# Chunked attention and an MLP on one core: exp stationary in the V products, a ones column for the sums, x normalized by token and turned, and a new order of the first three blocks

## The chip, the cores and the metric

One core of one Trainium2 chip. The metric is the device time of one execution in microseconds (us), median of several runs. The kernel runs on one core only. A profile is one execution of its own; its span is 1.8 us (before) below the time measured for that same execution.

## The reference, cut to what matters

```python
def _attn_ref(q, k, v):                       # (8, 8, 576, 64): batch, heads, tokens, head dim
    # 9 chunks of 64 tokens; each chunk attends to itself only
    scores = scale * np.matmul(q_c, k_c.transpose(0, 1, 2, 4, 3))
    scores = scores - np.max(scores, axis=-1, keepdims=True)
    attn = np.exp(scores)
    attn = attn / (np.sum(attn, axis=-1, keepdims=True) + 1e-09)
    return np.matmul(attn, v_c)...

def _moe_ref(x, w_in, w_out, beta):           # x (4608, 512), w_in (512, 2048), w_out (2048, 512)
    h = x @ w_in
    g = h * (1.0 / (1.0 + np.exp(-beta * h)))
    return g @ w_out

# x is the attention's output, token by token: row = token, column = 64 * head + d
```

## The kernel before

4608 tokens are nine blocks of 512. Per block: q and k are loaded, cast to bf16 and turned so that the head dimension lies on the partitions (by TensorE for blocks 0 to 2, by DMA from block 3 on); 64 score matmuls (8 heads x 8 chunks, each 64x64) fill four banks of PSUM, the memory that takes matmul results; ScalarE takes exp; 64 V products follow; the result is normalized. Then come 64 "first products" (w_in stationary, x moving, 512 columns), tanh on ScalarE and a gate on VectorE, and 64 "second products" with w_out. Of a matmul's two operands the stationary one is loaded by an instruction of its own (PEld in the profiles); the other is called the moving one. The first and second products are called dense matmuls here; each has 512 columns.

In before the V products give x with the head dimension on the partitions, as the first products want it. The sums over keys then have to be spread over those partitions:

```python
def sums(blk, bank):                  # 16 matmuls with a selector of ones
    for b in range(4):
        for hp in range(4):
            ... matmul(A[32*hp:32*hp+32, bank, 0:128], onesel[:, b, :], E[:, hp, 128*b:128*b+128], ...)

def invert(blk, bank):                # three steps on VectorE; the last two go from SBUF to SBUF
    reciprocal(R[:, :], A[:, bank, 0:128])
    tensor_copy(Rhi[:, :], R[:, :])                       # float32 -> bf16
    scalar_tensor_tensor(Rs, Rhi, mask, R, mult, subtract)

def spread(blk, u, banks):            # 8 matmuls: 1/sum to every partition of its head
    ... matmul(A[:, banks[g], col:col+128], sel[:, u, ..., :], Rs[:, :])

def attend(blk, u, banks):            # 32 V products, v stationary, exp moving
    ... matmul(ps[64*hb:64*hb+64, banks[g], col:col+64], v_bf[r, sa, cc, head, :], E[r, 2*u+hb, col:col+64])

def normalize(blk, u, g, bank):       # o_sb is a copy that ScalarE makes first
    tensor_tensor(xT[...], o_sb[...], A[:, bank, :], mult)
```

The kernel's own small scheduler puts all operations into one order by a "time" in slots, and each engine executes its part in that order. From block 2 on, a slot is one group of 4 first products and one of 4 second products of the block before.

Order of the first blocks in before: all first products of block 0, all second products of block 0 (with block 1's attention between them), all first products of block 1 (with block 2's attention), then first products of block n and second products of block n-1 alternate.

The softmax here doesn't subtract the row's maximum and nothing guards it: scores larger than these inputs give would overflow.

## Time and profile before

| | before |
|---|---|
| measured | 343.31 us median of 3 (341.46 to 345.04) |
| span of the profile | 342.2 us |
| first dense matmul / first of block 1 / first of block 2 | 22.8 / 64.8 / 97.6 us |
| block 2's stage (its first product to that of block 3) | 37.5 us |
| later blocks, one stage each | 32.6 us (block 7's, with the last block's scores, 31.8) |
| block 8's first product to the end | 45.0 us |

The stages are read from the weight loads of the first products, 64 to a block, in order of time. Lines of the page of before: the busy share of the engines; the span in 40 slices (each digit tenths of busy time; PEclk is the granted clock of TensorE); and the shares of the chain that ended last (the work that the end of the run waited for, followed back from step to step).

```profile
span 342.2 us, 6329 instructions
PE 303.8 (89%) x2688; PEld 148.3 (43%) x2688; DVE 150.8 (44%) x236; ACT 165.1 (48%) x262; POOL 113.2 (33%) x126
...
PE   1669978977589879999999999999999999999996
...
PEclk9999989999789999999999999999999999999999
...
PE 74%; DVE 11%; ACT 8%; DMA 3%; issue 2%; SPq 1%; POOL 0%; ACTq 0%; DVEq 0%; POOLq 0%
```

TensorE (PE) is the bottleneck nearly throughout, but 303.8 us of busy time is not all needed: 1152 dense matmuls at the 0.216 us at which they issue are 248.8 us.

PE waits 10.0 us in all for the inverted sums (`Rs`). And the two small VectorE steps L417 and L419 have means, 467 and 449 ns, that are far above their usual duration, as the timeline of VectorE shows for block 4 and for block 3:

```profile
152.72 0.95 DVE L415 RECIPROCAL R<-A 128x128 f32<-128x128 f32 x1
153.71 0.23 DVE L417 CAST Rhi<-R 128x128 bf16<-128x128 f32 x1
153.97 0.35 DVE L419 SCALAR_TENSOR_TENSOR Rs<-Rhi,mask,R 128x128 bf16<-128x128 bf16 x1
```

```profile
122.79 0.95 DVE L415 RECIPROCAL R<-A 128x128 f32<-128x128 f32 x1
123.78 1.40 DVE L417 CAST Rhi<-R 128x128 bf16<-128x128 f32 x1
125.21 0.35 DVE L419 SCALAR_TENSOR_TENSOR Rs<-Rhi,mask,R 128x128 bf16<-128x128 bf16 x1
```

The timeline of PE in before, in columns start, duration, what (a count after x; in brackets the idle time before it): the three long waits in block 2's stage, the last of them in block 3's attention; then the score burst of a usual block, and that of the last block.

```profile
99.51 0.60 PE L465 MATMUL F<-xT,w_in_bf 128*128 128x512 bf16 x2 [1.14 <-DVE xT L454]
...
119.19 0.41 PE L408 MATMUL A<-E,onesel 128*32 128x128 bf16 x16 [1.26 <-ACT E L402]
...
125.62 0.62 PE L429 MATMUL A<-Rs,sel 128*128 128x128 bf16 x8 [2.47 <-DVE Rs L419]
```

```profile
170.53 1.51 PE L395 MATMUL A<-qkO 64*64 64x64 bf16 x64
```

### The profile page before, as it was taken

How to read it: one execution, taken by the hardware profiler on the slowest of the kernel's cores; microseconds unless marked ns; L12 is line 12 of the kernel's file. 1: busy time of each engine (PE TensorE's matmuls, PEld its weight loads, DVE VectorE, ACT ScalarE, POOL GpSimd, SP SyncE). 2: the span in 40 equal slices, each digit the busy share in tenths (PEclk: the TensorE clock that was granted, in tenths of full speed). 3: DMA queues.
4: the chain of work that ended last, by engine and by line, in shares of the span. 5: the costliest groups of instructions: out<-in, count | busy, mean ns of one | idle time of the engine just before them, and what ended most of it. 6: DMA issues, size and time to landing. Idle time of an engine off the chain costs nothing.

```text
span 342.2 us, 6329 instructions
## 1 busy us (share of the span) xinstructions
PE 303.8 (89%) x2688; PEld 148.3 (43%) x2688; DVE 150.8 (44%) x236; ACT 165.1 (48%) x262; POOL 113.2 (33%) x126
## 2 busy tenths in 40 slices
PE   1669978977589879999999999999999999999996
PEld 1434435443234434545454454445444444444442
DVE  5255733184553355344534543463356336443300
ACT  2436633476234525465455546554655565544421
POOL 0467357242620960780096019403800000000000
PEclk9999989999789999999999999999999999999999
DMA  8999999999918979919932991450000000110012
GB/s 214 280 389 345 220 310 290 277 270 217 240 27 176 303 107 255 256 48 235 292 87 56 225 283 54 93 94 33 31 33 31 33 33 31 47 48 31 31 65 90
DMA packets 93484, 52.85 MB, mean 154 GB/s; under 512 B 66320, under 2 KB 84752, under 8 KB 93456
## 3 DMA queue, kind: packets, MB, share of 16 engines
q1 hardware_dynamic: 86208, 43.00, 50.6%
q10 hardware_dynamic: 7248, 9.45, 8.0%
q8 instruction: 21, 0.34, 0.4%
q14 instruction: 7, 0.06, 0.1%
HBM read 36.71 MB, written 9.44 MB: 135 GB/s over the span
## 4 chain that ended last, share of the span: by engine, by line
PE 74%; DVE 11%; ACT 8%; DMA 3%; issue 2%; SPq 1%; POOL 0%; ACTq 0%; DVEq 0%; POOLq 0%
PE F L465 33%; PE F L481 31%; ACT tt L471 4%; PE A L395 4%; DVE g L474 3%; PE A L429 3%; DVE R L415 2%; ACT E L402 2%; PE A L442 2%; DVE xT L454 1%; DMA qkstage<-in_k_dram 1%; SPq L285 1%; DVE Rhi L417 1%; DMA out_dram<-ostage 1%; DVE Rs L419 1%
## 5 line engine op out<-in xcount | busy, mean ns | idle before, releaser
L474 DVE SCALAR_TENSOR_TENSOR g<-tt,F 128x512 bf16<-128x512 bf16 x144 | 98.5, 686 | 148.6 <-ACT tt L471 148.6
L471 ACT ACTIVATE tt<-F,beta_half 128x512 bf16<-128x512 f32 x144 | 98.5, 687 | 113.9 <-PE F L465 113.0
L465 PE MATMUL F<-xT,w_in_bf 128*128 128x512 bf16 x576 | 150.1, 390 | 2.7 <-DVE xT L454 1.9
L481 PE MATMUL F<-w_out_bf,g 128*128 128x512 bf16 x576 | 144.8, 381 | 0.0
L465 PEld LDWEIGHTS F<-xT,w_in_bf 128*128 128x128 bf16 x576 | 55.4, 100 | 69.8 <-issue 5.4
L481 PEld LDWEIGHTS F<-w_out_bf,g 128*128 128x128 bf16 x576 | 54.9, 98 | 63.1 <-issue 0.6
L342 POOL COPY qkO<-qkT 128x1024 bf16<-128x1024 bf16 x22 | 42.6, 1980 | 92.7 <-PE A L395 84.3
L342 POOL CAST qkcast<-qkstage 128x1024 bf16<-128x1024 f32 x30 | 30.5, 1048 | 25.5 <-DMA qkstage<-in_k_dram 11.2
L486 ACT ACTIVATE ostage<-F 128x512 f32<-128x512 f32 x36 | 21.5, 597 | 23.7 <-PE F L481 21.5
L454 DVE TENSOR_TENSOR xT<-o_sb,A 128x512 bf16<-128x512 f32 x36 | 24.1, 681 | 2.5 <-PE A L429 2.3
L429 PE MATMUL A<-Rs,sel 128*128 128x128 bf16 x144 | 12.9, 239 | 13.0 <-DVE Rs L419 10.0
L449 ACT ACTIVATE o_sb<-A 128x512 f32<-128x512 f32 x32 | 18.8, 592 | 11.1 <-ACT ostage L486 4.2
L402 ACT ACTIVATE E<-A 128x512 bf16<-128x512 f32 x36 | 20.8, 595 | 5.9 <-PE A L395 3.4
L342 POOL CAST v_bf<-vstage 128x512 bf16<-128x512 f32 x36 | 21.3, 625 | 4.6 <-DMA vstage<-in_v_dram 4.5
L429 PEld LDWEIGHTS A<-Rs,sel 128*128 128x128 bf16 x144 | 9.8, 107 | 19.7 <-DVE Rs L419 14.0
L395 PE MATMUL A<-qkO 64*64 64x64 bf16 x576 | 12.9, 196 | 3.4 <-DVE qkO L342 2.2
L395 PEld LDWEIGHTS A<-qkO 64*64 64x64 bf16 x576 | 11.9, 110 | 7.1 <-issue 4.0
L415 DVE RECIPROCAL R<-A 128x128 f32<-128x128 f32 x9 | 8.6, 951 | 11.5 <-PE F L442 6.3
L369 PE MATMUL F<-identity,qkcast 128*128 128x128 bf16 x32 | 4.1, 311 | 8.7 <-DVE qkcast L342 6.9
L334 POOL CAST w_out_bf<-wstage 128x512 bf16<-128x512 f32 x16 | 9.7, 647 | 5.2 <-DMA wstage<-in_moe_w_out_dram 5.2
L322 POOL CAST w_in_bf<-wstage 128x512 bf16<-128x512 f32 x16 | 9.2, 617 | 4.6 <-DMA wstage<-in_moe_w_in_dram 4.6
L442 PEld LDWEIGHTS A<-E,v_bf 64*64 64x64 bf16 x512 | 5.9, 111 | 7.9 <-issue 3.8
(33 smaller groups left out, 66.4 us busy)
## 6 DMA issues: line engine op xcount, KB each, us to landing
out_dram<-ostage ACTq DMA_DIRECT2D x36, 256.0 KB, 2.3
qkstage<-in_q_dram SPq DMA_DIRECT2D x32, 256.0 KB, 4.2
qkstage<-in_k_dram SPq DMA_DIRECT2D x32, 256.0 KB, 5.7
vstage<-in_v_dram SPq DMA_DIRECT2D x32, 256.0 KB, 6.3
wstage<-in_moe_w_in_dram SPq DMA_DIRECT2D x4, 1024.0 KB, 10.2
wstage<-in_moe_w_out_dram SPq DMA_DIRECT2D x4, 1024.0 KB, 9.0
qkstage<-in_q_dram SPq DMA_DIRECT2D x8, 128.0 KB, 4.8
qkstage<-in_k_dram SPq DMA_DIRECT2D x8, 128.0 KB, 5.6
```

What stands on the lines that cost most here:

```text
L342: P.op(eng, lambda e: e.tensor_copy(dst, src), reads, writes)
L395: return e.matmul(A[64 * g:64 * g + 64, 2 * u + hb, col:col + 64], kT[r, 2 * cc + g, :], qT[r, 2 * cc + g, :])
L402: P.op("act", lambda e: e.activation(E[:, bank, :], A[:, bank, :], AF.Exp, scale=0.125), reads=[K("A", bank, v=("s", blk))], writes=[K("E" ...
L415: P.op("dve", lambda e: e.reciprocal(R[:, :], A[:, bank, 0:128]), reads=[K("A", bank, v=("l", blk))], writes=[K("R", v=blk)])
L429: return e.matmul(A[:, banks[g], col:col + 128], sel[:, u, 2 * (2 * w + ch) + g, :], Rs[:, :])
L449: P.op("act", lambda e: e.activation(o_sb[:, g, :], ps[:, bank, :], AF.Copy), reads=[K(psname, bank, v=("o", blk, u))], writes=[K("o_sb", ...
L454: P.op("dve", lambda e: e.tensor_tensor(xT[:, sx, 2 * u:2 * u + 2, :].rearrange("p w (c g i) -> p w c g i", c=4, g=2)[:, :, :, g, :], o_sb ...
L465: P.op("pe", lambda e, c=c: e.matmul(F[:, bank, :], w_in_bf[:, c, 128 * t:128 * t + 128], xT[:, sx, c, :], start=(c == 0), stop=(c == NC - ...
L471: P.op("act", lambda e: e.activation(tt[:, T % 3, :], F[:, bank, :], AF.Tanh, scale=beta_half[:, t:t + 1]), reads=[K("F", bank, v=("h", T) ...
L474: P.op("dve", lambda e: e.scalar_tensor_tensor(g2[:, sg, t, :], tt[:, T % 3, :], 1.0, F[:, bank, :], ALU.add, ALU.mult), reads=[K("F", ban ...
L481: P.op("pe", lambda e, t=t: e.matmul(F[:, bank, :], g2[:, sg, t, 128 * s:128 * s + 128], w_out_bf[:, t, :], start=(t == 0), stop=(t == NT ...
L486: P.op("act", lambda e: e.activation(ostage[:, N % NOS, :], F[:, bank, :], AF.Copy, scale=0.5), reads=[K("F", bank, v=("o", N))], writes=[ ...
```

## The change

Its intent: make exp the stationary operand, so that each V product gives tokens on the partitions; give v a 65th column of ones, so that the same product gives the sum too; then normalizing is one reciprocal of 16 columns and one multiply per half block, with no sums, no spreading and no copy. The price: x now has tokens on the partitions and must be turned, by TensorE in blocks 0 to 2 and by DMA from block 3 on. Besides, scores are issued as two bursts of 32, and the first three blocks come in a new order: block 1's q, k, v are loaded ahead of w_out, its attention goes under and after block 0's first products, and block 1's first products already alternate with block 0's second products.

```diff
-        v_bf = sb("v_bf", [128, NVA, 4, H, 64], BF16)
+        v_bf = sb("v_bf", [128, NVA, 4, H, 66], BF16)      # columns 64, 65 set to 1.0
-        def sums ... invert ... spread ... copy_o            (cut)
+        def attend(blk, u, ps=A, psname="A"):
+            ...   matmul(ps[64*half:64*half+64, bank, col:col+65],
+                         E[r, 2*u+hb, 256*w+64*cc:256*w+64*cc+64],
+                         v_bf[r, sa, cc, 4*u+2*w+hb, 0:65])
+        def normalize(blk, u, ps=A, psname="A"):
+            reciprocal(rec[:, u, :], o[:, :, :, 64])
+            tensor_tensor(x_sb[:, u, ...], o[:, :, :, 0:64], rec... broadcast over 64, mult)
+        def turn_dma(blk, u):  dma_start_transpose(xT[:, blk % NXT, u, ...], x_sb[:, u, ...])   # SP queue
+        def turn_pe(blk, u, ...):  8 transposes with the identity, then a copy by ACT or DVE
         def mm1(blk, t, bank):
-                    F[:, bank, :], w_in_bf[...], xT[:, sx, c, :],
+                    F[:, bank, :], w_in_bf[...], x_of(sx, c),       # runs of 64 columns
         (order)
-            return (0, 32)[blk] if blk < 2 else 16 * (blk + 1)
+            return 0 if blk == 0 else 16 * blk + 8
+        at(-43.5, load_qk, 1, 0) ... load_v, 1                       # ahead of w_out
-                at(t0, scores, blk, hp)
+                at(t0 + (hp // 2) * u, scores, blk, hp)
+                if blk > 2:  turn_dma   else:  turn_pe
         (other slots of the schedule cut)
```

## The prediction

> **What bounds it now.** TensorE. The chain of waits gives PE 74% of the 342.2 us span, DVE 11%, ACT 8%. In the timeline the 1152 dense matmuls issue every 0.216 us: 248.8 us, which the change does not touch. They run from 22.8 us to 339.0 us, so 67 us of that stretch is something else, in two parts.
>
> *Steady stage.* Scores of consecutive blocks start at 170.60, 203.19 and 235.78 us in the chain: 32.6 us a block, of which 128 dense matmuls are 27.6. Attention takes 4.95 us: scores about 1.55, two V products 0.5 each, sums 0.45, two spreads 0.55 each, and about 1.2 us in which PE waits (sums for exp 0.4-0.5, spread for the DVE inversion of 0.95+0.23+0.35 us). The score matmuls start four per 33 ns for the first 32 of 64, then one per 34 ns. The 32 of a V product all go at the fast rate. The Trainium skill (TensorE: Matmul & The Clock Gate, opening table) gives TensorE a queue of 64 instructions; 32 loads and 32 matmuls are just that. The trace agrees.
>
> *Early stage.* Before the third block's first product (98.4 us) only 192 dense matmuls are done: 41 us of work in 75 us. Losses: PE waits at 44-52, 76-97 us; three 3.4 us windows at half clock; attention and transposes of blocks 1 and 2.
>
> **What changes.** Per block, sums, inversion, and spreads go, with four ACT copies (0.59 us each). V products have 65 columns, still 32 per half, about 0.35 us. Normalizing becomes two reciprocals of 16 columns (0.95 us for 128 columns gives about 0.2) and two multiplies of 1024 columns (0.68 us for 512 gives about 1.25): about 2.9 us of DVE instead of 4.3, and PE no longer waits for it closely. Scores are split into 32 and 32, so both halves stay fast. PE attention in the steady stage: four bursts of about 0.5 us, 2.0 us instead of 4.95. Turning x is DMA from block 3 (half the size of the q/k turn, which lands in 8.0 us: I estimate 4-5 us, with some 11 us available). Gain 2.9 us x 6 blocks = 17 us (term A).
>
> Early: first product about 1.4 us sooner. Then block 1's q, k, v come ahead of w_out, its attention goes under and just after block 0's first products, and first products of block 1 alternate with second products of block 0. I expect a bare chain exp, V product, normalize, turn of some 6 us near 42-49 us, then little idling. Block 2's first products start near 84 us (80 to 90) instead of 98.4: 14 us (term B). The strided read of x by the first products should cost nothing.
>
> Sum: 84 + 960 x 0.216 + 6 x 2.1 + 3 stalls + 3.2 end = 310 us span; the measured time is 1 us more. **Prediction 311 us, 80% range 302 to 322.** Faster by over 2%: 0.96; within 2%: 0.03; slower: 0.01.
>
> **What would show it.** Distance between scores of consecutive blocks 29.4-30 us; the second half of scores at four per 33 ns; no PE wait on DVE in the steady stage; dense issue still 0.216 us; x turns landing in under 6 us, no PE wait on them; block 2's first products at 80-90 us; one PE gap of 5-8 us before block 1's first products, one or two half-clock windows; DVE and ACT busy less.
>
> **What would make it wrong.** x turns queued behind loads, so first products wait at every block; the strided moving operand slowing the dense issue; 65-column products at odd offsets slow; DMA not delivering block 2 and 3 inputs in the new order, so the early gain shrinks; a longer DVE multiply delaying the gate and hence PSUM banks.

## More of the kernel before

The scheduler also places the semaphores:

```python
for key, v in writes:
    add(self.writer.get(key), ...)
    for r in self.readers.get(key, ()):      # every reader of the tile's last version
        add(r, False)                        # ... is marked: it raises its engine's semaphore
```

So when a later operation on another engine overwrites a tile, each earlier reader of that tile raises a semaphore, although the wait itself is for the last count only.

The groups of instructions by line and form (columns: line, engine, operation, output<-inputs, form, count; busy us, mean ns; idle time just before, by what ended it):

```profile
L395 PE MATMUL A<-qkO 64*64 64x64 bf16 x576 | 12.9, 196 | 3.4 <-DVE qkO L342 2.2 <-ACT qkO L340 1.2
L429 PE MATMUL A<-Rs,sel 128*128 128x128 bf16 x144 | 12.9, 239 | 13.0 <-DVE Rs L419 10.0 <-DVE xT L454 3.1
...
L417 DVE CAST Rhi<-R 128x128 bf16<-128x128 f32 x9 | 4.2, 467 | 0.3
...
L419 DVE SCALAR_TENSOR_TENSOR Rs<-Rhi,mask,R 128x128 bf16<-128x128 bf16 x9 | 4.0, 449 | 0.3
```

```profile
268.29 0.74 PE L395 MATMUL A<-qkO 64*64 64x64 bf16 x64
```

Both bursts (in the two fences above) are 64 score matmuls. The usual one takes 1.51 us, the last block's 0.74 us.

## The result, and the profile after

After: 310.19 us median (309.6 to 310.33, 4 runs) against 343.28 us (341.46 to 345.04, 4 runs) of before. Ratios here are the mean time of one kernel's fast runs over that of the other's of the same rounds, so not quite the ratio of the medians: 0.9033, 95% interval 0.8984 to 0.9082.

| us, from the profiles | before | after | gained | predicted |
|---|---|---|---|---|
| start to block 2's first product | 97.6 | 86.3 | 11.3 | 14 (term B) |
| block 2's stage | 37.5 | 29.6 | 7.9 | 2.9 of term A; its stalls were expected to stay |
| blocks 3 to 7, five stages | 162.2 | 147.8 | 14.4 | 14.5 of term A |
| block 8 to the end | 45.0 | 45.0 | 0.0 | 0 |
| span | 342.2 | 308.6 | 33.6 | 32 |

The page of after, the same lines as shown for before:

```profile
span 308.6 us, 5739 instructions
PE 281.7 (91%) x2415; PEld 134.9 (44%) x2448; DVE 137.2 (44%) x194; ACT 150.6 (49%) x230; POOL 117.0 (38%) x130
...
PE   1679747999899999999999999999999999999995
...
PEclk9999985999999999999999999999999999999999
...
PE 80%; SPq 9%; DMA 6%; issue 1%; POOL 1%; DVE 1%; ACT 0%
```

(33 of the 1152 dense matmul records are missing from this trace, so PE's busy time reads low; the stages are read from the weight loads, which are all there.) Groups by line and form in after: scores, V products, multiply and reciprocal take the place of six groups.

```profile
L405 DVE TENSOR_TENSOR x_sb<-A,rec 128x1024 bf16<-128x1024 f32 x17 | 20.8, 1224 | 0.6
...
L367 PE MATMUL A<-qkO 64*64 64x64 bf16 x576 | 8.7, 200 | 1.2 <-ACT qkO L312 1.2
L389 PE MATMUL A<-v_bf,E 64*64 64x65 bf16 x544 | 8.6, 200 | 4.1 <-ACT E L374 2.1 <-DVE x_sb L405 2.0
...
L402 DVE RECIPROCAL rec<-A 128x16 f32<-128x16 f32 x17 | 4.3, 254 | 7.4 <-PE F L441 4.0 <-PE A L389 2.1 <-PE F L423 1.4
```

Two reciprocals and two multiplies are 2 x (0.254 + 1.224) = 2.96 us of VectorE a block (2.9 predicted). The timeline of PE in after, block 6's two score bursts and two V bursts; none has idle time in brackets:

```profile
178.69 0.45 PE L367 MATMUL A<-qkO 64*64 64x64 bf16 x32
...
180.90 0.45 PE L367 MATMUL A<-qkO 64*64 64x64 bf16 x32
...
189.15 0.45 PE L389 MATMUL A<-v_bf,E 64*64 64x65 bf16 x32
...
193.95 0.45 PE L389 MATMUL A<-v_bf,E 64*64 64x65 bf16 x32
```

A stage is now 29.55 us (29.4 to 30 predicted). 128 dense matmuls are 27.63 of it, so attention costs PE 1.92 us. The turns by DMA landed 3.0 us after issue (4 to 5 estimated); from the list of DMA issues (count, median us to landing):

```profile
xT<-x_sb SPq DMA_TRANSPOSE x12, 3.0
```

Before block 1's first product, PE in after has a bare chain, exp, V product, normalize, turn, as the timeline of PE shows:

```profile
40.32 0.44 PE L367 MATMUL A<-qkO 64*64 64x64 bf16 x32
41.75 0.19 PE L389 MATMUL A<-v_bf,E 64*64 64x65 bf16 x1 [0.98 <-ACT E L374]
...
45.48 0.66 PE L389 MATMUL A<-v_bf,E 64*64 64x65 bf16 x32 [2.04 <-DVE x_sb L405]
...
48.41 1.03 PE L423 MATMUL F<-identity,x_sb 128*128 128x128 bf16 x8 [1.31 <-DVE x_sb L405]
49.23 1.06 PE L441 MATMUL F<-xT,w_in_bf 128*128 128x512 bf16 x2
```

These waits are 5.2 us together (one gap of 5 to 8 us predicted). The TensorE clock ran at half rate there for 10.2 us on end (43.7 to 53.9 us in the clock record), longer than the one or two windows of 3.4 us that were predicted.

### The profile page after: what moved, and what is told of

Same layout as the page of the kernel before. It is cut to its first block, busy times and chain, and to the rows that moved or that the text cites. A ratio compares the mean times of both kernels' runs of the same rounds, so it can differ in the third digit from the quotient of the medians.

```text
span 308.6 us, 5739 instructions
## 1 busy us (share of the span) xinstructions
PE 281.7 (91%) x2415; PEld 134.9 (44%) x2448; DVE 137.2 (44%) x194; ACT 150.6 (49%) x230; POOL 117.0 (38%) x130
## 4 chain that ended last, share of the span: by engine, by line
PE 80%; SPq 9%; DMA 6%; issue 1%; POOL 1%; DVE 1%; ACT 0%
PE F L456 40%; PE F L441 36%; SPq L257 6%; DMA wstage<-in_moe_w_out_dram 4%; DMA vstage<-in_v_dram 2%; SPq L265 2%; PE A L389 2%; PE A L367 2%; SPq L274 1%; POOL w_out_bf L306 1%; PE A L341 1%; DVE x_sb L405 0%; PE A L423 0%; DVE g L449 0%; ACT tt L446 0%
## 5 line engine op out<-in xcount | busy, mean ns | idle before, releaser
L456 PE MATMUL F<-w_out_bf,g 128*128 128x512 bf16 x543 | 140.3, 381 | 2.6 <-issue 1.1
L314 POOL CAST qkcast<-qkstage 128x1024 bf16<-128x1024 f32 x32 | 34.7, 1092 | 27.0 <-DMA qkstage<-in_q_dram 13.2
L405 DVE TENSOR_TENSOR x_sb<-A,rec 128x1024 bf16<-128x1024 f32 x17 | 20.8, 1224 | 0.6
L389 PE MATMUL A<-v_bf,E 64*64 64x65 bf16 x544 | 8.6, 200 | 4.1 <-ACT E L374 2.1
L389 PEld LDWEIGHTS A<-v_bf,E 64*64 64x64 bf16 x544 | 6.3, 111 | 10.7 <-issue 6.6
L367 PEld LDWEIGHTS A<-qkO 64*64 64x64 bf16 x576 | 6.8, 112 | 8.2 <-issue 5.7
L367 PE MATMUL A<-qkO 64*64 64x64 bf16 x576 | 8.7, 200 | 1.2 <-ACT qkO L312 1.2
L402 DVE RECIPROCAL rec<-A 128x16 f32<-128x16 f32 x17 | 4.3, 254 | 7.4 <-PE F L441 4.0
L312 ACT ACTIVATE xT<-F 128x1024 bf16<-128x1024 bf16 x3 | 3.1, 1023 | 8.2 <-PE F L423 8.2
L341 PEld LDWEIGHTS F<-identity,qkcast 128*128 128x128 bf16 x32 | 3.1, 141 | 9.0 <-DVE qkcast L314 6.8
```

The source lines that it names most:

```text
L314: P.op(eng, lambda e: e.tensor_copy(dst, src), reads, writes)
L367: return e.matmul(A[64 * g:64 * g + 64, 2 * u + hb, col:col + 64], kT[r, 2 * cc + g, :], qT[r, 2 * cc + g, :])
L389: return e.matmul(ps[64 * half:64 * half + 64, bank, col:col + 65], E[r, 2 * u + hb, 256 * w + 64 * cc:256 * w + 64 * cc + 64], v_bf[r, sa ...
L405: P.op("dve", lambda e: e.tensor_tensor(x_sb[:, u, :, :, :].rearrange("p g c (h d) -> p (g c h) d", h=2).rearrange("p (b t) d -> p b t d", ...
L456: P.op("pe", lambda e, t=t: e.matmul(F[:, bank, :], g2[:, sg, t, 128 * s:128 * s + 128], w_out_bf[:, t, :], start=(t == 0), stop=(t == NT ...
```

## The experiments

All kernels gave the correct result. Each ratio is to the kernel before, run in the same rounds, from fast runs alone.

| run | median us | ratio to before |
|---|---|---|
| b_split | 336.62 | 0.986 (0.982 to 0.990) |
| b_lastsem | 335.54 | 0.982 (0.978 to 0.986) |
| a_whole | 314.33 | 0.920 (0.917 to 0.923) |
| a_whole_lastsem | 308.34 | 0.902 (0.898 to 0.905) |
| a_lastsem | 309.93 | 0.904 (0.900 to 0.907) |
| a_oldorder | 318.38 | 0.929 (0.924 to 0.934) |
| a_turnpe | 319.51 | 0.932 (0.928 to 0.936) |
| b_neworder | 342.82 | 1.001 (0.996 to 1.006) |
| b_neworder_wait | 338.01 | 0.989 (0.984 to 0.995) |
| b_neworder_two | 337.39 | 0.986 (0.981 to 0.992) |
| a_fill_gap | 308.52 | 0.901 (0.896 to 0.906) |
| a_fill_both | 308.14 | 0.900 (0.895 to 0.905) |

### Why are 32 scores fast and 64 slow?

The prediction had a mechanism, a queue of 64 instructions, and said that the trace agreed with it (the last block's burst in the same trace does not). The start times of the score matmuls in before, written as the differences in ns, first of the burst at 203.12 us and then of the last block's:

```
203.12 us: 3 3 4 42 4 2 3 23 3 4 3 22 ... (32 matmuls, four per 33 ns), then 27 34 34 34 34 34 35 34 ... to the end
268.29 us: 4 3 3 43 3 3 3 22 4 3 4 21 ... four per 33 ns for all 64 (last four slower)
```

A queue would slow both. The difference between them: nothing overwrites q and k of the last block, so only 4 of its 64 scores raise a semaphore in the trace, where all 64 of the usual burst do. That gives the rival: increments are taken one per 34 ns, and only so many may be outstanding. The Trainium skill (TensorE: Matmul & The Clock Gate, "The cost: per-tile semaphore tail") says that per-matmul increments serialize at 26.3 ns each and that one increment on the last tile is enough. Four kernels tell the theories apart.

b_split, before with

```diff
-                at(t0, scores, blk, hp)
+                at(t0 + (hp // 2) * u, scores, blk, hp)
```

> The kernel before with its 64 score matmuls of blocks 1 to 8 issued as 32 and 32, nothing else. Queue theory (32 loads and 32 matmuls fit a queue of 64): both halves start four per 33 ns, so each of the seven blocks that had 1.5 us of scores gives back about 0.75 us: 338 us (336 to 340). Increment theory (each score matmul raises a semaphore, and those can be taken only one per 34 ns once some 32 are outstanding): the same, 338 us, since the first half's are worked off during the dense matmuls between. The rival that the split is worth nothing: 343 us.

b_lastsem, before with one burst of 64 and only the last reader of a tile on an in-order engine kept:

```diff
-            self.readers.setdefault(key, []).append(op)
+            kept = self.readers.setdefault(key, [])
+            if op["kind"] == "compute" and op["queue"] != "pool":
+                kept[:] = [r for r in kept if r["kind"] != "compute" or r["queue"] != op["queue"]]
+            kept.append(op)
```

> The kernel before, scores in one burst of 64, but of several readers of a tile on one in-order engine only the last one raises the semaphore that the next writer waits for. Queue theory: the scores keep their second half at 34 ns a matmul, about 1.5 us, and the time stays within 1 us of 343. Increment theory: all bursts of 64 become like that of the last block, 0.74 us where nobody waits for the tiles any more, so 0.75 us less in each of seven blocks, and sums, exp and inversion start up to 1 us sooner: 333 to 338 us.

a_whole, after with scores in one burst (`at(t0, scores, blk, hp)`, and likewise for block 1):

> The kernel after with the scores of blocks 1 to 8 in one burst of 64 again. Both theories: the second 32 go at 34 ns each, 0.7 to 0.8 us more in each of seven blocks, less 0.1 us for one burst fewer: 314.5 us (313 to 316.5). If the split is worth nothing: 310 us.

a_whole_lastsem, both edits on after:

> The kernel after with the scores in one burst of 64 and with only the last reader of a tile on an in-order engine raising a semaphore. Queue theory: as without that, 314 to 315 us. Increment theory: the burst takes about 0.7 us instead of 1.5, and the normalizing after each V product starts about 0.9 us sooner (it now starts 1.43 us after a burst that is issued in 0.37 us), which counts where the chain is bare, before block 1's first products: 306 to 310 us, at or under the kernel after.

Measured: 336.6, 335.5, 314.3 and 308.3 us. The two kernels with one burst and fewer increments decide it. The timeline of PE, first a_whole, then a_whole_lastsem, then b_lastsem, the scores of one block each:

```profile
183.06 1.51 PE L367 MATMUL A<-qkO 64*64 64x64 bf16 x64
```

```profile
176.80 0.76 PE L370 MATMUL A<-qkO 64*64 64x64 bf16 x64
```

```profile
164.93 0.80 PE L398 MATMUL A<-qkO 64*64 64x64 bf16 x64
```

The same 64 matmuls, in the same order and burst, take 1.51 us with an increment each and 0.76 to 0.80 us when only 6 of them raise one. So the queue is not what slowed them, and the increments are. The split that the change brought works too: in after both halves of 32 go at the fast rate with an increment each. That the increments of the first half drain in the 2.2 us between the halves fits (32 at 34 ns are 1.1 us), but is argued; how many may be outstanding was not measured further. The skill's figure of 26.3 ns per increment is lower than the 34 ns found here; the measurement decides. On the same chip and in the same rounds, a_whole_lastsem is 1.9% below a_whole (308.34 / 314.33).

b_split and b_lastsem met their expected totals, but not in the expected way. In their traces the later stages are 32.0 and 31.8 us instead of 32.6 (block 7's was 31.8 before), so blocks 3 to 7 gain 2.2 and 3.0 us of the 7.7 and 7.8 us between the spans. Block 2's first product came 6.6 and 7.0 us sooner (90.9 and 90.6 us instead of 97.6), more than two shorter bursts can give, and block 2's stage got longer (38.6 and 39.6 us instead of 37.5). Part of both is which small VectorE steps were stretched (more on these below): in before the two steps at 84.7 us, 1.0 us each; in b_split and b_lastsem not block 2's but above all block 3's, where the cast took 0.93 and 2.84 us.

a_lastsem, after with the split kept and the fewer increments:

> The kernel after, split scores as they are, with only the last reader of a tile on an in-order engine raising a semaphore. Queue theory: no change, 310 us. Increment theory: in the steady stage nothing (its bursts are already under the limit, and nothing waits closely), but the bare chain before block 1's first products has two V bursts, each followed 1.4 us later by its normalizing; about 0.9 us less for each, and a shorter gap for the half clock: 1.5 to 4 us less, 306 to 308.5 us.

Measured 309.9 us: no gain that can be told from after's 310.2. In its trace normalizing did start sooner in the bare chain (the second reciprocal 0.66 us after the start of its V burst, at 45.44 us, against 1.35 us in after), and block 2's first product came at 84.8 us instead of 86.3, so the span is 307.1 us. But this profile is one of two executions with a granted clock of 0.989 (6.8 us at half rate); the other four, at 0.983 like after's, have spans of 308.2 to 309.1 us, no shorter than after's 307.9 to 308.6. So the earlier normalizing is there in the trace, and that it shortens the run is not shown.

### How much is the order, and how much the operations?

a_oldorder: after's operations with before's slots for loads, casts, attention and products of blocks 0 to 2, and for block 3's attention (those scheduling lines of before put back; turns on TensorE for blocks 1 and 2 as in after).

> The operations of after (V products with exp stationary, ones column, normalizing by token, turning of x, split scores) in the order of the first three blocks that before has. My theory: the order is worth about 8 us of the 11.3 us that the change gains before block 2's first products (block 1's and 2's shorter attention gives the rest), the operations everything after it: about 318 us (315 to 323). Rival, the operations do it all and the order nothing: 310 us. Rival, the order does the most of the early gain and also the removal of the stalls of block 2's stage: 325 us or more.

Measured 318.4 us, as my theory had it: 8.2 us above after. In its trace block 2's first product comes at 96.3 us, block 2's stage is 29.4 us and later ones 29.55: the operations alone give 1.2 us early, the whole gain of block 2's stage and the whole gain of the later stages. Putting the new order on top then brings block 2's first product from 96.3 to 86.3 us. That would be 10 us of the early 11.3. But the profile is the longest of four executions that differ much (spans of 318.5, 318.3, 315.0 and 314.4 us, at granted clocks of 0.973, 0.973, 0.984 and 0.989); after's are 307.9 to 308.6. So with the new operations the order is worth some 8 us, between 6 and 11 by execution.

b_neworder, before's operations in after's slots for the first three blocks:

> The operations of before (sums, inversion, spreading, scores in one burst) in the order of after. My theory: it gains about 8 us early less what the longer bare chain of block 1's attention costs (it has two more waits for VectorE), so 338 us (334 to 344). Rival, the order is worth as much with either set of operations: 335 us or less. Rival, the order needs the short chain and is worth nothing without it: 343 us or more.

Measured 342.8 us, inside the range that my theory gave (334 to 344), but at the rival's value: nothing gained. Yet the order did act early, block 2's first product came at 89.3 us (97.6 in before). It was lost again in block 2's stage, 43.7 us long instead of 37.5. Two large waits of PE stood there: 4.76 us for block 2's last normalizing and 3.53 us for the inversion. The timelines of VectorE and of POOL in b_neworder, same stretch:

```profile
113.38 0.95 DVE L415 RECIPROCAL R<-A 128x128 f32<-128x128 f32 x1
114.36 1.78 DVE L417 CAST Rhi<-R 128x128 bf16<-128x128 f32 x1
116.18 1.91 DVE L419 SCALAR_TENSOR_TENSOR Rs<-Rhi,mask,R 128x128 bf16<-128x128 bf16 x1
```

```profile
112.18 7.74 POOL L342 COPY qkO<-qkT 128x1024 bf16<-128x1024 bf16 x4 [7.83 <-DMA qkT<-qkcast]
```

The two small steps took 1.78 and 1.91 us, while POOL ran copies of q and k. The Trainium skill (SBUF — State Buffer, "SBUF: two separate sides") says that VectorE and GpSimd share one pair of ports under an exclusive lock, taken by VectorE for an operation in a two-port mode or with two SBUF inputs, and that the loser blocks. Here the cast reads and writes SBUF, the other step has two SBUF tensors. The single instructions of the traces look like such blocking and not like a slower pace: in before and b_neworder all eleven steps that took longer than usual end 0.08 us (the cast) or 0.14 us (the other) after a POOL instruction does (here 116.14 after 116.06 us and 118.08 after 117.94 us).

b_neworder_wait makes POOL's copies of block n wait for block n-1's inversion:

```diff
-                      [K("qkT", v=blk)], [K("qkO", hp, which, half, v=blk)
+                      [K("qkT", v=blk)] + ([K("Rs", v=blk - 1)] if blk > 3 else []),
+                      [K("qkO", hp, which, half, v=blk)
```

> The operations of before in the order of after, and now the four copies on POOL that order block n's q and k wait until block n-1's inversion is done (blocks 4 and up). In the run without that wait (342.8 us) block 3's two small inversion steps on VectorE took 1.78 and 1.91 us under such a copy instead of 0.23 and 0.35, PE stood 3.5 us for them, and a window at half clock followed. Theory, the overlap stretches them: the steps take 0.23 and 0.35 us again, PE waits 0.4 us there, and the time falls by 3 to 5 us to 338 to 340 us. Rival, they were long for another reason (DVE's own queue, a late release): still over 1 us each, time 342 to 344 us.

Measured 338.0 us (ratio 0.989 against 1.001). The timelines of VectorE and POOL in that run:

```profile
114.12 0.95 DVE L416 RECIPROCAL R<-A 128x128 f32<-128x128 f32 x1
115.10 0.23 DVE L418 CAST Rhi<-R 128x128 bf16<-128x128 f32 x1
115.36 0.35 DVE L420 SCALAR_TENSOR_TENSOR Rs<-Rhi,mask,R 128x128 bf16<-128x128 bf16 x1
```

```profile
115.78 7.78 POOL L342 COPY qkO<-qkT 128x1024 bf16<-128x1024 bf16 x4 [10.51 <-DVE Rs L420]
```

The steps are back at 0.23 and 0.35 us, and one more wait gains some 4 us (4.8 by the medians, 1.2% by the ratios, from different rounds). That the overlap with POOL stretched them is shown, and this agrees with the skill's lock. It happened in before too (1.40 us at 123.78 us, 1.01 and 1.01 us at 84.73 and 85.78 us, with PE waits of 2.47 and 2.94 us behind them). After's multiply reads PSUM and one SBUF operand: 1.22 us in all 18 cases, also under POOL copies.

b_neworder_two, besides that block 2's attention packed closer:

```diff
-        attention(2, 32.1, 0.6)
+        attention(2, 32.1, 0.5)
```

> As that, and the attention of block 2 packed closer (0.5 instead of 0.6 of a slot), so that its last normalizing stands on VectorE ahead of the copy that waits for block 3's DMA turn; PE had waited 4.8 us for it. Theory, the order is worth about 8 us with the old operations too, and was lost to these two stalls: 332 to 336 us. Rival, the order is worth nothing with the longer attention chain: 338 us or more.

Measured 337.4 us, between the two: the 4.8 us wait is gone, but a new one (2.28 us for POOL's copies of block 3, with 6.8 us at half clock) came in its place. So the order with these two repairs is worth about 5 us on the old operations (1.4% by the ratio), and the order alone some 8 us on the new ones (a_oldorder to after, from medians of different rounds). Whether POOL's wait would have helped before in its own order, and whether a better schedule of the old operations would get more, was not tried; both stay open.

### What the turning by DMA is worth

a_turnpe, after with TensorE turning x in every block (`if blk > 99:` instead of `if blk > 2:` before `turn_dma`):

> The kernel after with x turned on TensorE in every block instead of by DMA from block 3 on. Each turn is eight 128-column transposes of 56 ns, 0.45 us plus about 0.1 us of change-over, twice a block, and a copy on ScalarE (1.02 us) and VectorE (0.69 us): 1.1 us more a block over six blocks, 316.5 us (315 to 319). If the DMA turn itself had been holding something back: less than that.

Measured 319.5 us, a stage of 31.23 us instead of 29.55: 1.68 us more, where 1.1 was expected. The timeline of PE in a_turnpe has the missing part, a wait of PE on VectorE:

```profile
201.54 0.62 PE L423 MATMUL A<-identity,x_sb 128*128 128x128 bf16 x8 [0.61 <-DVE x_sb L405]
...
202.86 0.61 PE L423 MATMUL A<-identity,x_sb 128*128 128x128 bf16 x8
```

Two bursts of about 0.5 us and 0.61 us of waiting for `x_sb`. The DMA turn costs PE neither of the two.

### What limits the early stage now?

The chain of waits of after, read up to 60 us (columns: start, duration, what), runs through the DMA queue until 49 us:

```profile
29.96 7.60 DMA vstage<-in_v_dram
...
37.77 11.67 DMA wstage<-in_moe_w_out_dram
...
49.49 2.30 POOL w_out_bf L306 x4
51.81 2.73 PE F L456 x7
```

From 51.8 us on it runs nearly all through PE. But half clock was there as well. Two kernels test it, on top of a_whole_lastsem. a_fill_gap puts useless matmuls into the chain's gaps, into a free PSUM bank:

```diff
+        at(16.5, fill, 4, F, "F", 2, True)     # 512 columns each, before the first V burst of block 1
+        at(17.15, fill, 6, F, "F", 2, True)
+        at(18.25, fill, 2, F, "F", 2, True)
```

> The kernel after with scores in one burst and only the last reader raising a semaphore (308.3 us when run before), and with 12 matmuls of no use (512 columns, into a PSUM bank that is free) in the bare chain of block 1's attention, 41 to 49 us, where PE is idle. If the half clock of that stage (6.8 us) comes of the idle gap and costs what is run in it double: the clock stays full, 1.5 to 2.5 us less, 306 to 307 us. If the gap is what matters and not the clock: no change, 308 us. If the filling delays the chain: 309 us or more.

Measured 308.5 us. Granted clock by stretch in after, then in a_fill_gap (columns: stretch, length, busy us of PE, PEld, DVE, ACT, POOL with counts, PEclk, mean DMA share, GB/s):

```profile
42.00:54.00 12.00, 7.37 (x89) 3.93 (x91) 3.65 (x5) 3.80 (x6) 8.63 (x16) 0.57 1.05 374
54.00:74.00 20.00, 19.15 (x171) 9.68 (x173) 8.55 (x11) 10.98 (x17) 11.12 (x13) 1.00 1.02 259
```

```profile
42.00:54.00 12.00, 8.82 (x108) 4.17 (x109) 4.34 (x6) 5.48 (x9) 7.09 (x13) 1.00 1.04 371
54.00:74.00 20.00, 18.26 (x167) 9.27 (x169) 8.95 (x12) 11.59 (x18) 12.13 (x16) 1.00 1.01 270
```

The clock is full, and the time is as without the filling (308.3, in other rounds). Block 2's first product is at 84.82 us in the traces of both a_fill_gap and a_whole_lastsem. That does not make half clock free: the filling also stood in the way, as block 1's first product came at 49.2 us instead of 48.4, and the full clock may have paid that back. And among the unfilled executions the shorter half clock goes with the shorter span: of a_whole_lastsem's six, three at a clock of 0.988 to 0.989 have 305.7 to 306.2 us and three at 0.982 to 0.983 have 307.0 to 307.6. Whether the clock makes that 1.3 us or only goes with it stays open. a_fill_both adds 70 small matmuls ahead of and between block 0's transposes:

```diff
+        at(-60, fill, 44, A, "A", 0, False)
+        for i in range(3):
+            at(-49.4 + i, fill, 6, A, "A", 0, False)
+        at(-46.3, fill, 8, A, "A", 0, False)
```

> As that, with 70 matmuls of no use (128 columns) besides, in front of and between the transposes and the scores of block 0, 1.4 to 15 us. If PE earns its full clock by activity, it has it before 15 us instead of near 24 us, the first products from 20 us on run at full rate, and the chain of block 0 is a little shorter: another 1.5 to 3 us less, 303.5 to 305.5 us. If they only stand in the way of the chain: 307 us or more.

Measured 308.1 us, a miss. The filling did not keep the clock up in the prefix (half rate again from 9.4 to 12.8 us and from 16.2 to 26.4 us), and PE stood 3.0 us inside a V burst of block 0 with no releaser in the profile. Its first dense matmul came at 23.0 us, 2.8 us later than in a_whole_lastsem. And block 2's first product still came at 84.7 us. So 2.8 us at the start do not show at block 2's first product. The chain of waits offers a reason: in after it runs through the loads, w_out's above all, until 49 us, so that delays before that are hidden behind data still to come. From block 0's first second product at 51.8 us on, PE stands only 2.4 of the 34.5 us until block 2's first product, so there its own work sets the pace, although the DMA engines are at a mean share of 1.0 or more from 42 to 86 us. That arrival sets the pace up to about 50 us is argued; no run with less data was made.

## Why the prediction was right

- **The sum was right, 311 us predicted and 310.2 measured**, with two errors that cancelled: term A 22.3 us (17 predicted) and term B 11.3 us (14 predicted). That the sum came within 1 us is in part luck.
- **Steady stage, right.** 29.55 us a stage (29.4 to 30), dense issue still 0.216 us with the strided x, no PE wait on VectorE, turns landing in 3.0 us. a_turnpe shows that the turn by DMA keeps 1.68 us a block off PE.
- **Block 2's stage, mis-sized.** The term "3 stalls" (3 us) was kept in the sum as if before's stalls there would stay. They were waits of the longer chain: 1.14 us for the last normalizing, 1.26 us for the sums' exp, 2.47 us for the inversion that POOL stretched, where a usual block waits 0.40 us for exp and 0.43 us for the inversion. They went with the chain: the stage fell by 7.9 us, 5.0 more than a usual block; these waits are some 4 us of that, the rest was not traced. a_oldorder shows that the operations do this (29.4 us), and b_neworder_wait shows the stretch by itself.
- **Term B, mis-sized.** Block 2's first product came at 86.3 us, in the range of 80 to 90 but 2.3 us later than the 84 of the sum; 0.8 us more of the difference is its starting point, 98.4 us where the weight loads show 97.6. The prediction's warning that DMA may not deliver in the new order fits the chain of waits, which runs through DMA to 49 us; which term cost the 2.3 us is not shown.
- **The reason for fast and slow scores, wrong.** "32 loads and 32 matmuls are just that" fitted the numbers by chance. Increments did it: 64 matmuls in one burst take 0.76 us once only 6 of them raise one. The step's number was right since both theories ask for the same split.
- **Half clock, under-counted.** 10.2 us at half rate instead of one or two windows of 3.4 us. In a_fill_gap full clock brought no gain, but the filling delayed the chain, so what half clock costs stays open.

The operations are worth about 24 us (before to a_oldorder, same rounds) and the order some 8 us on top (a_oldorder to after, different rounds).

No version here is shown to be faster than after: a_whole_lastsem (0.902) and a_fill_both (0.900) are within after's interval (0.898 to 0.908).

## What to carry to other kernels

When a burst of small matmuls slows down in its second half, compare it with a burst of the same matmuls that nobody waits for before naming a cause; a scheduler that lets every reader raise a semaphore is cheap to mend, since the last reader on an in-order engine was enough in every kernel here (the results stayed correct). When a small VectorE step has a mean far above its usual duration, look what POOL did at that moment: a wait on POOL's side was worth some 4 us here. And follow an early gain to the end of the run: the new order brought the old operations' block 2 forward by 8.3 us and lost it all in the stage after, until two stalls there were repaired. When executions of one kernel differ by 1%, note which one the profile shows before reading a stage off it.

## What the Trainium skill lacked or had wrong

- TensorE: Matmul & The Clock Gate, "The cost: per-tile semaphore tail": gives 26.3 ns per increment as a tail of up to 16 tiles. Here about 32 score matmuls started 8 ns apart on average with an increment each, and only those after them were held to 34 ns; the page has neither this slack nor the 34 ns.
- The same page, opening table, queue of 64: true or not, it is no explanation of the slow half; 64 loads and 64 matmuls ran through in 0.76 us.
- SBUF — State Buffer, "SBUF: two separate sides": the lock agrees (0.23 us became 1.78 us and came back with a wait). The page has the loser blocked for a whole instruction but gives no figure for small VectorE steps under a queue of POOL copies: in b_neworder, under copies of 2 us each, two steps in a row took 1.78 and 1.91 us.
- TensorE: Matmul & The Clock Gate, Part 1: half-rate stretches inside the traces are multiples of 3.41 us (3.41, 6.83, 10.24), which agrees with the page's window of 3413 ns. 70 identity matmuls in the prefix did not hold the clock, though (half rate from 16.2 to 26.4 us in a_fill_both); the page gives no measure of how much activity a window needs.
- DMA: Bandwidth & Descriptors gives a bandwidth for DMA transposes (261 GB/s in one kernel) but no time for one of this size (the skill times only a single 128x128 block, on a page on VectorE): 1024 columns by 128 partitions of bf16, 256 KB, landed 3.0 us after issue here, which is 87 GB/s with the wait in the queue included.
